# Instance normalization on one core: statistics halves summed on GpSimd, an early Sqrt table load, and g/b loads on ScalarE's queue

## The chip, the cores and the metric

The kernel runs on one core of one Trainium2 chip. The metric is the device time of one execution in microseconds. The profiler's span, from the first to the last instruction, is a little shorter than that time: 94.7 us for the kernel before, in a run of 96.55 us. All times below that belong to a point of the run count from the start of the span.

Names: VectorE is DVE, ScalarE is ACT, GpSimd is Pool, SyncE is SP. "Transfers" are the 16 DMA engines of the core.

## What is computed

Input x has shape (32, 576, 16, 32) in bf16: 32 x 576 = 18,432 images of 512 values. Each image is normalized by its own mean and variance and then scaled and shifted by its channel's g and b:

```python
mu = x.mean(axis=(-2, -1), keepdims=True)
var = ((x - mu) * (x - mu)).mean(axis=(-2, -1), keepdims=True)
xhat = (x - mu) / jnp.sqrt(var + 1e-5)
return xhat * g.reshape(1, -1, 1, 1) + b.reshape(1, -1, 1, 1)
```

x is 18.9 MB, and so is the output. Each value is read from HBM once and written once.

## The kernel before

**Tiling.** The 18,432 images are laid over 128 partitions, 144 images to a partition. A tile is one image on each partition: 128 x 512 bf16, 131 KB. All 144 tiles stay in SBUF, in the tensor `xs`, from the load to the store; nothing is evicted, and a tile is normalized in place.

**Loads.** SP issues 12 loads of 2, 2, 4, 8 and then 16 tiles each (table `ic`). Each has its own semaphore. Behind the first of them SP issues the loads of g and b, 36 KB each (L274, L275).

**Batches.** The tiles go in 13 batches of 3 to 18 tiles (table `bs`). The stages of one batch are:

1. Statistics, tile by tile. Most tiles go to DVE: `bn_stats` (L331) writes six numbers per image, a count, a mean and a sum of squared deviations for the even elements and again for the odd ones; `bn_aggr` (L333) turns the six into mean and variance in `mv`. The first `ka` tiles of a batch go to ACT instead: `p1` (L340) sums a tile with the accumulator, `p2` (L342) sums the squared deviations, and one small ACT operation per batch, `tiny` (L346), scales the means.
2. One Sqrt on ACT for the whole batch (L348), then one reciprocal on DVE (L335).
3. Three small operations on Pool, `tt1` to `tt3` (L353, L355, L357), which make `scale` = rstd x g and `bias` = b - mean x scale.
4. The normalization x scale + bias of each tile, on one of three engines: `na` tiles of a batch on ACT (L350), `nd` on DVE (L337), the rest on Pool (L359).
5. One store for the batch, which SP issues when all its tiles are normalized (L289).

**Order.** Each engine runs its instructions in the order in which they stand in its queue. The order isn't written out by hand. `build_ops` makes a list of operations with what each depends on; `simulate` is a small planner that runs through this list when the program is built, with a duration for each kind (`COST`), an arrival time for each load (`in_chunk_arrivals`) and a priority for each kind (`PRIO`), and puts each engine's operations in the order in which they would start. `emit_engine` then writes the instructions in that order. Where an operation depends on another, it waits for that engine's semaphore to reach the count of the operation that it needs. An instruction that waits holds up everything behind it on its engine.

The stores share SP's queue with the loads. All loads are issued by 9 us, before the first store at 12.48 us, and the transfers take them up in that order; so the first half of the run reads and the second half writes.

Of the kernel before, what the change touches and what calls it, by code (L numbers as in the profile page):

```python
# [9 lines left out]

COST = dict(
    bnstats=(594, 594), bnaggr=(68, 80), recip=(130, 252), normD=(323, 323),
    p1=(612, 612), p2=(705, 705), tiny=(190, 250), sqrt=(115, 216), normA=(702, 702),
    tt=(197, 222), normP=(742, 742),
)
NORM_CONTENDED = 785
HANDOFF = 90
HANDOFF_SAME = 100
DMA_TILE_NS = 306
DMA_FIRST = 1050  # L20
DMA_ISSUE = 380
DMA_SEM = 250
PRIO = dict(sqrt=0, tiny=1, recip=0, tt=0, bnaggr=2, normA=3, p2=4, p1=5, bnstats=5, normP=5, normD=6)


class Op:
    __slots__ = ("eng", "kind", "tile", "batch", "deps", "chunk", "busy", "lat", "start", "end", "done", "idx", "sub")

    def __init__(self, eng, kind, tile=None, batch=None, deps=(), chunk=None, sub=None):
        self.eng, self.kind, self.tile, self.batch = eng, kind, tile, batch  # L30
        self.deps = list(deps)
        self.chunk = chunk
        self.sub = sub
        key = "tt" if kind.startswith("tt") else kind
        self.busy, self.lat = COST[key]
        self.start = self.end = self.done = None
        self.idx = None

    def __repr__(self):
        return f"{self.eng}:{self.kind}(t={self.tile},b={self.batch})@{self.start}"  # L40


def in_chunk_arrivals(in_chunks, t0=0.0, n_pre_dmas=0):
    arr = []
    dma_free = 0.0
    issue_t = t0 + n_pre_dmas * DMA_ISSUE
    for (lo, hi) in in_chunks:
        issue_end = issue_t + DMA_ISSUE
        start = max(issue_t + DMA_FIRST, dma_free)
        end = start + (hi - lo) * DMA_TILE_NS  # L50
        dma_free = end
        arr.append(end + DMA_SEM)
        issue_t = issue_end
    return arr, dma_free, issue_t


def build_ops(n_tiles, batches, in_chunks):
# [5 lines left out]
    stat_done = {}  # L63
    for b, B in enumerate(batches):
        lo, hi, ka = B["lo"], B["hi"], B["ka"]
        p1s = []
        for i in range(lo, lo + ka):
            o1 = Op("A", "p1", tile=i, batch=b, chunk=chunk_of[i])
            o2 = Op("A", "p2", tile=i, batch=b, deps=[o1])
            ops += [o1, o2]  # L70
            p1s.append(o1)
            stat_done[i] = o2
        for i in range(lo + ka, hi):
            o1 = Op("D", "bnstats", tile=i, batch=b, chunk=chunk_of[i])
            o2 = Op("D", "bnaggr", tile=i, batch=b, deps=[o1])
            ops += [o1, o2]
            stat_done[i] = o2
        stats = [stat_done[i] for i in range(lo, hi)]
        tiny = None
        if ka > 0:  # L80
            tiny = Op("A", "tiny", batch=b, deps=p1s)
            ops.append(tiny)
        sq = Op("A", "sqrt", batch=b, deps=stats)
        rc = Op("D", "recip", batch=b, deps=[sq])
        t1 = Op("P", "tt1", batch=b, deps=[rc])
        t2 = Op("P", "tt2", batch=b, deps=[t1] + ([tiny] if tiny else []))
        t3 = Op("P", "tt3", batch=b, deps=[t2])
        ops += [sq, rc, t1, t2, t3]
        B["ops"] = dict(tiny=tiny, sqrt=sq, recip=rc, tt1=t1, tt2=t2, tt3=t3)
# [18 lines left out]
def simulate(ops, arrivals, t_start=0.0, verbose=False):  # L108
# [6 lines left out]

    def ready_time(o):
        r = t_start
        if o.chunk is not None:
            r = max(r, arrivals[o.chunk])
        for d in o.deps:  # L120
            if d.start is None:
                return None
            r = max(r, d.done + (HANDOFF_SAME if d.eng == o.eng else HANDOFF))
        return r

    n_left = len(ops)
    while n_left:
        best = None
        for e in "DAP":
            cands = []  # L130
            for o in pending[e]:
                r = ready_time(o)
                if r is not None:
                    cands.append((r, o))
            if not cands:
                continue
            tstar = max(free[e], min(r for r, o in cands))
            avail = [(PRIO["tt" if o.kind.startswith("tt") else o.kind], o.tile if o.tile is not None else -1, o.batch, r, o)
                     for r, o in cands if r <= tstar + 1e-9]
            avail.sort(key=lambda x: (x[0], x[2], x[1]))  # L140
            o = avail[0][4]
            if best is None or tstar < best[0]:
                best = (tstar, e, o)
        assert best is not None, "deadlock in schedule construction"
# [6 lines left out]
        o.start = tstar  # L151
        o.end = tstar + busy
        o.done = tstar + lat
# [12 lines left out]
def plan(n_tiles, batch_sizes, ka_list, na_list, nd_list, in_chunk_sizes, out_groups=None, verbose=False):  # L166
    batches = []
    lo = 0
    for G, ka, na, nd in zip(batch_sizes, ka_list, na_list, nd_list):
        batches.append(dict(lo=lo, hi=lo + G, ka=ka, na=na, nd=nd))  # L170
        lo += G
# [3 lines left out]
    for s in in_chunk_sizes:  # L175
        in_chunks.append((lo, lo + s))
        lo += s
    assert lo == n_tiles
    arrivals, dma_in_end, sp_free = in_chunk_arrivals(in_chunks, n_pre_dmas=0)
    ops = build_ops(n_tiles, batches, in_chunks)  # L180
    engs, free = simulate(ops, arrivals)
    if out_groups is None:
        out_groups = [(B["lo"], B["hi"]) for B in batches]
    norm_of = {}
# [5 lines left out]
    for (lo, hi) in out_groups:  # L190
# [9 lines left out]
    res = dict(batches=batches, in_chunks=in_chunks, arrivals=arrivals, engs=engs, free=free,  # L200
               out=out_info, total=total, dma_in_end=dma_in_end, out_groups=out_groups)
    return res


# [6 lines left out]
DEFAULT_TABLE = dict(  # L211
    bs=[3, 7, 10, 11, 15, 17, 18, 15, 15, 13, 12, 4, 4],
    ka=[2, 1, 2, 2, 4, 4, 4, 4, 4, 2, 2, 0, 0],
    na=[1, 2, 1, 1, 6, 4, 9, 5, 7, 7, 5, 1, 1],
    nd=[0, 0, 0, 0, 0, 0, 0, 0, 0, 0, 4, 3, 3],
    ic=[2, 2, 4, 8, 16, 16, 16, 16, 16, 16, 16, 16],
)


def bass_standalone__instancenorm__sampling_kernel(nc, x, g, b, out, table=None, NJUNK=4):  # L220
# [4 lines left out]
    assert NI % P == 0  # L225
# [5 lines left out]
    pl = plan(n, tb["bs"], tb["ka"], tb["na"], tb["nd"], tb["ic"], out_groups=tb.get("og"))  # L231
# [3 lines left out]
    out_groups = pl["out_groups"]  # L235

    c1 = -1.0 / (S * math.sqrt(S))
    c2 = 1.0 / math.sqrt(S)
    c3 = -math.sqrt(S)
# [4 lines left out]
    with ExitStack() as es:  # L244
# [8 lines left out]
        nms = sb("nms", [P, n], FP32)  # L253
# [4 lines left out]
        bias = sb("bias", [P, n], FP32)  # L258

# [4 lines left out]
        out_sem = sem("out_sem")  # L264
        block = es.enter_context(nc.Block())

        @block.sync
        def _(sp):
            gsrc = bass.AP(g.tensor, 0, [[0, P // q], [n, q], [1, n]])
            bsrc = bass.AP(b.tensor, 0, [[0, P // q], [n, q], [1, n]])  # L270
            for c, (lo, hi) in enumerate(in_chunks):
                sp.dma_start(xs[:, lo:hi, :], xv[:, lo:hi, :]).then_inc(in_sem[c], 16)  # L272
                if c == 0:
                    sp.dma_start(g_sb[:], gsrc).then_inc(g_sem, 16)  # L274
                    sp.dma_start(b_sb[:], bsrc).then_inc(b_sem, 16)  # L275
            norm_of = {}
            for Bt in batches:
                norm_of.update(Bt["norm"])
# [13 lines left out]
        def emit_engine(eng, E):  # L292
# [11 lines left out]
            for o in ops:  # L304
                assert o.idx == ops.index(o) if False else True
# [10 lines left out]
                lo, hi = Bt["lo"], Bt["hi"]  # L316
                i = o.tile
# [18 lines left out]
                elif k == "normD":  # L336
                    ins = eng.tensor_scalar(xs[:, i, :], xs[:, i, :], scale[:, i:i + 1], bias[:, i:i + 1],  # L337
                                            AluOpType.mult, AluOpType.add)
                elif k == "p1":
                    ins = eng.activation(jb, xs[:, i, :], ACTF.Identity, scale=c1, accum_out=nms[:, i:i + 1])  # L340
                elif k == "p2":
                    ins = eng.activation(jb, xs[:, i, :], ACTF.Square, bias=nms[:, i:i + 1], scale=c2,  # L342
                                         accum_out=mv[:, i, 1:2])
                elif k == "tiny":
                    ka = Bt["ka"]
                    ins = eng.activation(mv[:, lo:lo + ka, 0], nms[:, lo:lo + ka], ACTF.Identity, scale=c3)  # L346
                elif k == "sqrt":
                    ins = eng.activation(std[:, lo:hi], mv[:, lo:hi, 1], ACTF.Sqrt, bias=eps, scale=1.0)  # L348
                elif k == "normA":
                    ins = eng.activation(xs[:, i, :], xs[:, i, :], ACTF.Identity, bias=bias[:, i:i + 1],  # L350
                                         scale=scale[:, i:i + 1])
                elif k == "tt1":
# [5 lines left out]
                elif k == "normP":  # L358
                    ins = eng.tensor_scalar(xs[:, i, :], xs[:, i, :], scale[:, i:i + 1], bias[:, i:i + 1],  # L359
                                            AluOpType.mult, AluOpType.add)  # L360
                else:
                    raise AssertionError(k)
# [6 lines left out]
        @block.scalar  # L369
        def _(act):  # L370
            emit_engine(act, "A")

        @block.gpsimd
        def _(pool):
            emit_engine(pool, "P")
# [28 lines left out]
```

## Time and profile before

The median of three runs is 96.42 us (96.40 to 96.67).

| row | count | busy us | mean ns |
|---|---|---|---|
| DVE bn_stats (L331) | 113 | 73.9 | 666 |
| DVE bn_aggr (L333) | 113 | 17.5 | 162 |
| DVE normalization (L337) | 10 | 3.7 | 424 |
| ACT p1 (L340) | 31 | 19.0 | 615 |
| ACT p2 (L342) | 31 | 21.9 | 707 |
| ACT normalization (L350) | 50 | 36.8 | 800 |
| ACT table loads (L340, L348) | 2 | 2.6 | 1283 |
| Pool normalization (L359) | 84 | 63.8 | 780 |
| Pool tt1, tt2, tt3 (L353, L355, L357) | 39 | 8.9 | 225 to 234 |

The engines are busy for 79.9 us (DVE, 84% of the span), 82.3 (ACT, 87%) and 71.6 (Pool, 76%). The queue that SP feeds takes 95.9% of the time of the 16 DMA engines.

How to read it: the mean of a row is the time of one instruction from its start to its end, and on DVE and ACT an instruction begins before the end of the one ahead of it. The distance from start to start, called the pitch below, is what an instruction costs in a queue. The timeline gives it: bn_stats 0.58 us and bn_aggr 0.08 on DVE, p1 0.61 and p2 0.70 on ACT, a normalization 0.70 on ACT and 0.75 on Pool.

### The profile page before, as it was taken

Reading aid. Unit: us, or ns where it says so; the run is one execution under the profiler, and the core shown is the slowest. Engines: PE = TensorE matmul, PEld = TensorE weight load, DVE = VectorE, ACT = ScalarE, POOL = GpSimd, SP = SyncE. Lnnn points to the kernel's source line nnn. Section 1 sums busy time; section 2 is a strip of 40 time slices with the busy share of each in tenths; the row PEclk is TensorE's granted clock in tenths of the full one; section 3 lists DMA queues with packets and bytes.
Section 4 is the critical chain, followed back from the end, with each engine's and each line's share of the span. In section 5 each row is a group of like instructions: output and inputs, shape, how many; then the busy total and the mean of one; then the engine's idle time right before and its main releaser. Section 6 shows DMA issues by size and latency. Waiting matters only on the chain.

```text
span 94.7 us, 659 instructions
## 1 busy us (share of the span) xinstructions
DVE 79.9 (84%) x249; ACT 82.3 (87%) x200; POOL 71.6 (76%) x127
## 2 busy tenths in 40 slices
DVE  0039597999999999999999999999999999999100
ACT  5598397989999999999999999999999999899000
POOL 0000807959999999999999999999999999895000
DMA  1799999999999999999999999999999999899995
GB/s 29 208 348 394 436 415 443 429 415 436 436 429 429 436 422 422 439 422 422 436 381 439 429 428 438 441 442 419 433 436 420 432 393 422 344 413 399 420 403 211
DMA packets 3894, 37.87 MB, mean 400 GB/s; under 512 B 689, under 2 KB 689, under 8 KB 1585
## 3 DMA queue, kind: packets, MB, share of 16 engines
q1 hardware_dynamic: 3888, 37.82, 95.9%
q14 instruction: 6, 0.04, 0.1%
HBM read 18.95 MB, written 18.87 MB: 399 GB/s over the span
## 4 chain that ended last, share of the span: by engine, by line
DVE 76%; DMA 12%; SPq 3%; issue 0%; DVEq 0%; ACT 0%
DVE bnst L331 62%; DMA xs<-in_x_dram 12%; DVE mv L333 8%; DVE xs L337 3%; SPq L272 2%; DVE rstd L335 2%; SPq L274 1%; SPq L275 1%; DVEq L244 0%; ACT std L348 0%
## 5 line engine op out<-in xcount | busy, mean ns | idle before, releaser
L331 DVE BATCH_NORM_STATS2 bnst<-xs 128x6 f32<-128x512 bf16 x113 | 73.9, 666 | 7.9 <-DMA xs<-in_x_dram 7.9
L359 POOL TENSOR_SCALAR xs<-xs,scale,bias 128x512 bf16<-128x512 bf16 x84 | 63.8, 780 | 1.1
L350 ACT ACTIVATE xs<-xs,bias,scale 128x512 bf16<-128x512 bf16 x50 | 36.8, 800 | 1.0 <-POOL bias L357 0.9
L342 ACT ACTIVATE junk<-xs,nms 128x512 bf16<-128x512 bf16 x31 | 21.9, 707 | 0.0
L340 ACT ACTIVATE junk<-xs 128x512 bf16<-128x512 bf16 x31 | 19.0, 615 | 3.2 <-DMA xs<-in_x_dram 3.2
L333 DVE BATCH_NORM_AGGREGATE mv<-bnst 128x2 f32<-128x6 f32 x113 | 17.5, 162 | 0.1
L353 POOL TENSOR_TENSOR scale<-rstd,g_sb 128x15 f32<-128x15 f32 (+9 forms) x13 | 3.0, 230 | 12.7 <-DVE mv L333 12.5
L340 ACT ACTIVATION_READ_ACCUMULATOR junk<-xs 128x1 f32 x31 | 5.8, 187 | 0.0
L342 ACT ACTIVATION_READ_ACCUMULATOR junk<-xs,nms 128x1 f32 x31 | 5.8, 187 | 0.0
L337 DVE TENSOR_SCALAR xs<-xs,scale,bias 128x512 bf16<-128x512 bf16 x10 | 3.7, 424 | 0.0
L357 POOL TENSOR_TENSOR bias<-b_sb,tmp 128x15 f32<-128x15 bf16 (+9 forms) x13 | 2.9, 225 | 0.7
L355 POOL TENSOR_TENSOR tmp<-mv,scale 128x15 f32<-128x15 f32 (+9 forms) x13 | 3.0, 234 | 0.5
L348 ACT ACTIVATE std<-mv 128x15 f32<-128x15 f32 (+9 forms) x13 | 2.6, 200 | 0.4 <-DVE mv L333 0.4
L335 DVE RECIPROCAL rstd<-std 128x15 f32<-128x15 f32 (+9 forms) x13 | 2.8, 213 | 0.2 <-ACT std L348 0.2
L346 ACT ACTIVATE mv<-nms 128x2 f32<-128x2 f32 (+2 forms) x11 | 2.1, 195 | 0.0
L340 ACT ACT_TABLE_LOAD x1 | 1.3, 1283 | 0.7 <-PEq L389 0.7
L348 ACT ACT_TABLE_LOAD x1 | 1.3, 1283 | 0.0
L389 POOL MEMSET const-float32-0.0<- 128x1 f32 x1 | 0.1, 99 | 0.2 <-issue 0.2
L389 POOL MEMSET const-bfloat16-1.0<- 128x1 bf16 x1 | 0.1, 102 | 0.0
L389 POOL MEMSET const-uint8-127<- 128x1 uint8 x1 | 0.1, 102 | 0.0
L389 POOL MEMSET const-float32-1.0<- 128x1 f32 x1 | 0.1, 99 | 0.0
## 6 DMA issues: line engine op xcount, KB each, us to landing
xs<-in_x_dram SPq DMA_DIRECT2D x8, 2048.0 KB, 26.7
out_dram<-xs SPq DMA_DIRECT2D x3, 1920.0 KB, 9.8
out_dram<-xs SPq DMA_DIRECT2D x1, 2304.0 KB, 13.1
out_dram<-xs SPq DMA_DIRECT2D x1, 2176.0 KB, 15.5
out_dram<-xs SPq DMA_DIRECT2D x1, 1664.0 KB, 5.9
out_dram<-xs SPq DMA_DIRECT2D x1, 1536.0 KB, 5.5
out_dram<-xs SPq DMA_DIRECT2D x1, 1408.0 KB, 23.4
out_dram<-xs SPq DMA_DIRECT2D x1, 1280.0 KB, 28.2
```

The costliest lines, as they stand in the source:

```text
L331: ins = eng.bn_stats(bnst[:, i, :], xs[:, i, :])
L333: ins = eng.bn_aggr(mv[:, i, :], bnst[:, i, :])
L335: ins = eng.reciprocal(rstd[:, lo:hi], std[:, lo:hi])
L337: ins = eng.tensor_scalar(xs[:, i, :], xs[:, i, :], scale[:, i:i + 1], bias[:, i:i + 1], AluOpType.mult, AluOpType.add)
L340: ins = eng.activation(jb, xs[:, i, :], ACTF.Identity, scale=c1, accum_out=nms[:, i:i + 1])
L342: ins = eng.activation(jb, xs[:, i, :], ACTF.Square, bias=nms[:, i:i + 1], scale=c2, accum_out=mv[:, i, 1:2])
L348: ins = eng.activation(std[:, lo:hi], mv[:, lo:hi, 1], ACTF.Sqrt, bias=eps, scale=1.0)
L350: ins = eng.activation(xs[:, i, :], xs[:, i, :], ACTF.Identity, bias=bias[:, i:i + 1], scale=scale[:, i:i + 1])
L353: ins = eng.tensor_tensor(scale[:, lo:hi], rstd[:, lo:hi], g_sb[:, lo:hi], AluOpType.mult)
L355: ins = eng.tensor_tensor(tmp[:, lo:hi], mv[:, lo:hi, 0], scale[:, lo:hi], AluOpType.mult)
L357: ins = eng.tensor_tensor(bias[:, lo:hi], b_sb[:, lo:hi], tmp[:, lo:hi], AluOpType.subtract)
L359: ins = eng.tensor_scalar(xs[:, i, :], xs[:, i, :], scale[:, i:i + 1], bias[:, i:i + 1], AluOpType.mult, AluOpType.add)
```

## The change

It has four parts.

1. **bn_aggr is replaced for most batches.** For a batch marked "p" in a new table `agg`, the two halves that `bn_stats` wrote are put together for the whole batch at once, in six small operations. Pool adds the halves (`P1`: the sum of the means and of the squared deviations, in `pa`) and subtracts the means (`P2`: `dd`). ACT squares the difference with the right factor (`sq`: `qq`) and halves the sum of the means (`mh`). Pool adds `qq` and the summed squared deviations (`P4`). Sqrt then divides by the count through its scale. Batches marked "d" keep bn_aggr. ACT's own statistics tiles now write mean and summed squares in the form that this Sqrt takes, and `tiny` goes.
2. **The Sqrt table is loaded first.** Pool sets one value, and ACT takes its square root ahead of all else, so that the table set with Sqrt is loaded at the start and not at the first batch's Sqrt.
3. **g and b are loaded from ACT's queue**, behind that warm-up, and not from SP's between the first x loads.
4. **New tables and planner figures.** There are ten batches of 3 to 25 tiles in place of 13, other shares for the engines, loads of 1, 2, 4, 8, 17 and then 16 tiles, and a store for each batch as before. The planner's costs change a little, and it takes a load's semaphore as 1000 ns late in place of 250.

It is meant to relieve DVE of the aggregation, and to bring the first x loads and the first Sqrt forward.

```diff
 def build_ops(batches, in_chunks):
...
         for i in range(dlo, hi):
             o1 = Op("D", "bnstats", tile=i, batch=b, chunk=chunk_of[i])
...
+            if agg == "d":
+                o2 = Op("D", "bnaggr", tile=i, batch=b, deps=[o1])
...
+        if agg == "p":
+            if bns:
+                P1 = Op("P", "P1", batch=b, deps=bns)
+                P2 = Op("P", "P2", batch=b, deps=bns)
+                sq = Op("A", "sq", batch=b, deps=[P2])
+                mh = Op("A", "mh", batch=b, deps=[P1])
+                P4 = Op("P", "P4", batch=b, deps=[sq, P1])
...
+            sqr = Op("A", "sqrt", batch=b, deps=[P4] + p2s)
...
-DEFAULT_TABLE = dict(
-    bs=[3, 7, 10, 11, 15, 17, 18, 15, 15, 13, 12, 4, 4],
-    ka=[2, 1, 2, 2, 4, 4, 4, 4, 4, 2, 2, 0, 0],
-    na=[1, 2, 1, 1, 6, 4, 9, 5, 7, 7, 5, 1, 1],
-    nd=[0, 0, 0, 0, 0, 0, 0, 0, 0, 0, 4, 3, 3],
-    ic=[2, 2, 4, 8, 16, 16, 16, 16, 16, 16, 16, 16],
-)
+DEFAULT_TABLE = {"bs": [3, 11, 20, 25, 21, 17, 16, 16, 9, 6], "ka": [0, 0, 9, 4, 3, 3, 1, 1, 1, 0],
+                 "na": [1, 0, 5, 10, 8, 12, 10, 7, 3, 2], "nd": [0, 0, 0, 0, 0, 0, 0, 3, 6, 4],
+                 "agg": ["p", "d", "p", "p", "p", "p", "p", "p", "p", "d"],
+                 "ic": [1, 2, 4, 8, 17, 16, 16, 16, 16, 16, 16, 16]}
...
             for c, (lo, hi) in enumerate(in_chunks):
                 sp.dma_start(xs[:, lo:hi, :], xv[:, lo:hi, :]).then_inc(in_sem[c], 16)
-                if c == 0:
-                    sp.dma_start(g_sb[:], gsrc).then_inc(g_sem, 16)
-                    sp.dma_start(b_sb[:], bsrc).then_inc(b_sem, 16)
...
                 elif k == "p1":
-                    ins = eng.activation(jb, xs[:, i, :], ACTF.Identity, scale=c1, accum_out=nms[:, i:i + 1])
+                    ins = eng.activation(jb, xs[:, i, :], ACTF.Identity, scale=inv_s, accum_out=mv[:, i, 0:1])
...
+                elif k == "sq":
+                    ins = eng.activation(qq[:, dlo:hi], dd[:, dlo:hi], ACTF.Square, scale=sq_scale)
+                elif k == "mh":
+                    ins = eng.activation(mv[:, dlo:hi, 0], pa[:, dlo:hi, 0], ACTF.Identity, scale=0.5)
...
+                elif k == "P1":
+                    ins = eng.tensor_tensor(pa[:, dlo:hi, :], bnst[:, dlo:hi, 1:3], bnst[:, dlo:hi, 4:6], AluOpType.add)
+                elif k == "P2":
+                    ins = eng.tensor_tensor(dd[:, dlo:hi], bnst[:, dlo:hi, 1], bnst[:, dlo:hi, 4], AluOpType.subtract)
+                elif k == "P4":
+                    ins = eng.tensor_tensor(mv[:, dlo:hi, 1], qq[:, dlo:hi], pa[:, dlo:hi, 1], AluOpType.add)
...
         def _(act):
+            act.wait_ge(warm_sem, 1)
+            act.activation(warm[:, 1:2], warm[:, 0:1], ACTF.Sqrt)
+            if gb_q == "scalar":
+                gb_loads(act)
             emit_engine(act, "A")
...
         def _(pool):
+            pool.memset(warm[:, 0:1], 1.0).then_inc(warm_sem, 1)
...
             emit_engine(pool, "P")
```

## The prediction

> **What bounds the kernel now.** I read the busy slices first, because they show all engines and the transfers against one clock.
>
> ```profile
> DVE  0039597999999999999999999999999999999100
> ACT  5598397989999999999999999999999999899000
> POOL 0000807959999999999999999999999999895000
> DMA  1799999999999999999999999999999999899995
> ...
> HBM read 18.95 MB, written 18.87 MB: 399 GB/s over the span
> ```
>
> Each digit is 2.4 us. The chain of waits names VectorE for 76% of the span, but the transfers are busy earlier than VectorE and five slices longer. So I asked for the transfers by stretch:
>
> ```profile
> 2.00:5.00 3.00, 0.00 (x0) 1.58 (x6) 0.00 (x0) 1.00 0.76 201
> ...
> 20.00:48.00 28.00, 28.00 (x88) 28.00 (x77) 27.35 (x46) 1.00 1.01 429
> 48.00:52.00 4.00, 4.00 (x15) 4.00 (x15) 4.00 (x6) 1.00 0.98 408
> 52.00:77.00 25.00, 24.82 (x78) 24.84 (x56) 24.53 (x42) 1.00 1.01 433
> 77.00:83.00 6.00, 6.00 (x20) 5.75 (x11) 5.63 (x11) 1.00 0.87 370
> ```
>
> The columns are the stretch, its length, busy DVE, ACT and POOL, clock, transfer share and GB/s. The transfers run full (share 1.01) from 20 to 77 us: this is a DMA-bound kernel with two leaks. All loads stand in the queue by 9 us, so the reads run first. Summing the GB/s column by microsecond, 18.41 MB have moved at 47 us and the last read at about 48.25 us; then the writes run, at 131 KB / 433 GB/s = 0.303 us a tile. Ideally 144 tiles take 43.6 us, 91.9 us as the end. Data in fact ends at 93.6 us, and the leak is in 77 to 83 us: (433-370) x 6 / 433 = 0.9 us. The timeline shows why:
>
> ```profile
> 80.04 2.21 ACT L350 ACTIVATE xs<-xs,bias,scale 128x512 bf16<-128x512 bf16 x3
> ...
> 82.32 6.47 SPq L289 DMA_DIRECT2D out_dram<-xs  x4
> ```
>
> A 13-tile store was issued at 82.32, when ACT's last normalization of that batch ended at 82.25; its first bytes moved at 83.0. So **a batch that is ready later than 0.75 us before the previous store drains costs idle transfer time.** The engines matter through that alone. The other leak is the start:
>
> ```profile
> 1.18 0.61 SPq L274 DMA_DIRECT2D g_sb<-in_g_dram  x1
> 1.84 0.59 SPq L275 DMA_DIRECT2D b_sb<-in_b_dram  x1
> 2.47 6.75 SPq L272 DMA_DIRECT2D xs<-in_x_dram  x11
> ```
>
> The loads of g and b sit between the first and second x loads. From 3.00 to 4.25 us only 96 GB/s move, at a share of 0.60.
>
> **What the Trainium skill says.** "DMA: Bandwidth & Descriptors", section "Queues, rings and completion order": SP and ACT each have their own ring on the same 16 DMA engines, served in turn. So g and b on ACT's queue leave SP's issue order but not the DMA engines; the trace of before has no ACT queue to compare. "ScalarE: Activation LUTs", section "What ACT_TABLE_LOAD costs": 1283 ns; both loads here took 1283. "SBUF — State Buffer", section "Who interferes with whom": a DVE operation with at most one SBUF input outside the two-port modes does not contend with GpSimd. The trace agrees: bn_stats keeps 0.58 us a tile beside a busy Pool.
>
> **The change part by part.** *g/b off SP's queue, first chunk one tile.* The second x load issues at about 0.73+0.45 = 1.18 instead of 2.47, 1.29 us earlier. That is the most the stream can gain. Against it, the g/b packets now run inside the stream; 1.25 us x 0.60 = 0.75 us bounds their engine time, so the least is 0.54. I take 0.8. The g wait before Pool's first scale is about 8 us into the run; g landed 2.4 us after issue before, so even issued at 2.2 us (after the warm table load) it is there.
>
> *Table.* Sqrt's set is loaded first and serves Identity and Square: before, the second load ran at 6.9 us; after has one. Saves 1.28 us of ACT, worth nothing: ACT then waits for the fifth chunk, below.
>
> *Work moved.* The tables give 122 bn_stats (113), 17 bn_aggr (113), 13 DVE normalizations (10); 22 ACT statistics tiles (31), 58 ACT normalizations (50); 73 Pool normalizations (84), and 54 small Pool operations (39). By the pitches in the timeline (bn_stats 0.583, aggr 0.08, DVE norm 0.32; ACT 0.61+0.705 and 0.704; Pool 0.752): DVE +5.2-7.7+1.0 = -1.5, and about -2 with three fewer reciprocals; ACT -11.8+5.6, and 16 small operations more, 14 fewer at 0.11 (+0.2) = -6.0, -1.3 table; Pool -8.3 + 15 x 0.25 = -4.5. The changed scales of the ACT statistics and the write of the mean straight into its place cost nothing: same shapes. Three stores fewer (10 against 13) save SP's issues of 0.33 us, which lie beside running transfers. All three engines lose work. But the profile says busy time is not the measure; readiness against the stores is.
>
> *Where the engines start.* The order of the changed kernel has ka=0 in the first two batches: ACT gets one tile, then waits for the fifth chunk, ending at tile 32 in both kernels. DVE started on that chunk at 15.87 before; so 15.07 after. ACT then has 21 x 1.315 + 57 x 0.704 + 23 x 0.11 = 70.3 us, so it can't end before 85.4 (87.7 before). Pool: batch 1's reciprocal stands behind the first bn_stats of that chunk on DVE, so its scale starts at 15.8 and its normalizations at 16.7.
>
> *What is queued behind the new waits.* The new path per batch is Pool's two sums, ACT's Square, Pool's sum, Sqrt: four crossings. Each Pool sum stands behind up to six normalizations, and ACT's Square behind it holds ACT's normalizations. Walking the order with the pitches above (Pool sums 0.25, the pair 0.5; the nearest row is tmp at 230 ns; 128x42 might be 0.35) gives few stops: ACT about 1 us in all, Pool 1.3 at 26 us (scale behind a Sqrt that follows eight ACT tiles). Ready times, and stores from 47.45 (48.25-0.8), plus 0.2 for the dip at 48 to 52:
>
> | store (tiles) | last producer | ready | previous drained | lost | drained |
> |---|---|---|---|---|---|
> | 3 (25), tile 59 | Pool | 53.5 | 57.95 | 0 | 65.55 |
> | 4 (21) | Pool | 65.35 | 65.55 | 0.55 | 72.45 |
> | 5 (17) | Pool | 69.75 | 72.45 | 0 | 77.6 |
> | 6 (16) | ACT | 77.55 | 77.6 | 0.7 | 83.15 |
> | 7 (16) | ACT, DVE | 82.75 | 83.15 | 0.35 | 88.35 |
> | 8 (9) | DVE, ACT | 85.0 | 88.35 | 0 | 91.1 |
> | 9 (6) | ACT | 86.4 | 91.1 | 0 | 92.9 |
>
> "Lost" is ready + 0.75 - drained. Store 4's Pool line: 16.7 + 1.3 idle + 54 x 0.752 + 26 x 0.25 = 65.1, and 0.2 for the hand-offs. Store 6's ACT line: 15.07 + 21 x 1.315 + 45 x 0.704 + 18 x 0.11 = 76.35, and about 1 of stops, which the walk puts at 77.55. With 0.3 us of tail, as before (83.0 + 33 x 0.303 + 0.3 for the gap at 87 gives 93.3 against 93.6), data ends at 93.2. Sum: start -0.8; leaks of 1.6 instead of 0.9 and 0.3, +0.4. So 96.42 - 0.4 = **96.0 us**. The removed bn_aggr is thus worth almost nothing on the path: DVE gets nine more tiles, and ACT's normalizations end the stores.
>
> **The rivals.** *No wait at all*: the ready times are pessimistic by over 0.7 us, and the stream runs through: 47.45 + 0.2 + 43.6 + 0.3 = 91.55, 2.0 less: 94.4. For it: margins at all other stores and less work everywhere. Against: ACT's plain sum of work already gives store 6. *New hand-offs cost more*: an extra 0.1 us at each of 12 ACT crossings up to store 7 gives 1.2 more: 97.2, **slower**. For it: ACT now waits on Pool twice a batch, and Pool's spans in a profile are rough; against: the waits table of before puts ACT's wait on Pool at 0.9 us in all. *No gain at the start*: g/b on the second ring take as much from the small chunks as they took before, gain 0.1: 96.7.
>
> **How the numbers follow.** Main case 0.48 (95.4 to 96.5, by the start's 0.54 to 1.29 and pitches), no wait 0.19, hand-offs 0.23, no start gain 0.10. Faster: 0.36 + 0.19 + 0.01 = 0.56. Same (96.13 to 96.71): 0.12 + 0.01 + 0.06 = 0.19. Slower: 0.22 + 0.03 = 0.25. The range 94.5 to 97.2 leaves out about half of the no-wait case and the worse half of the hand-offs.
>
> **What would show it.** Right: transfers at full share from about 2 us; DVE's wait for the fifth chunk ends near 15.1; transfer share under 1 near 66, 78 and 83 us, each before a store whose issue follows Pool or ACT; last normalization near 86.4. Wrong: a full share to the end (then 94.4), or ACT idle over 2 us on Pool's sums (then slower), or the fifth chunk at 15.8.

## The result and the profile after

The changed kernel takes 95.26 us (median of 12 runs, 94.99 to 95.93). In the same comparison the kernel before takes 96.89 us at the median; the ratio is 0.9845, with a 95% interval of 0.9812 to 0.9878. That is about 1.5 us less. The forecast was 0.4 us less (96.0, range 94.5 to 97.2). The comparisons leave disturbed runs out; the profiles of experiments 4 and 13 are of such runs (97.76 and 97.54 us) and serve only to show when loads land and stores are issued.

The busy slices of the kernel after, 2.33 us to a digit in a span of 93.3 us:

```profile
DVE  0388898999999999999999999999999999994000
ACT  6020807999999999999999999999999999996000
POOL 1022602999929999999999999999999999630000
DMA  1999999999999999999999999999999999989996
```

The second digit of the transfers was 7 and is 9: they are full sooner. At the other end DVE shows no work in the last three slices, against the last two before: the engines are done a little further ahead of the last transfers.

The same stretches as in the prediction (stretch, length, busy DVE, ACT, POOL, clock, transfer share, GB/s):

```profile
2.00:5.00 3.00, 1.14 (x2) 0.22 (x2) 0.00 (x0) 1.00 0.92 266
...
20.00:48.00 28.00, 28.00 (x51) 28.00 (x76) 26.01 (x46) 1.00 1.00 427
48.00:52.00 4.00, 4.00 (x8) 4.00 (x11) 4.00 (x9) 1.00 1.05 443
52.00:77.00 25.00, 24.89 (x46) 24.97 (x49) 24.64 (x48) 1.00 1.00 430
77.00:83.00 6.00, 5.80 (x21) 6.00 (x13) 4.48 (x12) 1.00 0.97 414
```

The middle has not changed (429 to 427 and 433 to 430 GB/s). Both leaks are smaller: the start moves 266 GB/s for 201, and 77 to 83 us moves 414 for 370.

The issues at the start, and the two instructions that began on the fifth load (timeline):

```profile
0.73 6.97 SPq L307 DMA_DIRECT2D xs<-in_x_dram  x12
0.74 1.28 ACT L412 ACT_TABLE_LOAD   x1 [0.74 <-PEq L436]
0.87 0.62 ACTq L301 DMA_DIRECT2D g_sb<-in_g_dram  x1
1.52 0.62 ACTq L302 DMA_DIRECT2D b_sb<-in_b_dram  x1
...
14.77 0.63 ACT L371 ACTIVATE junk<-xs 128x512 bf16<-128x512 bf16 x1
```

```profile
14.77 0.69 DVE L362 BATCH_NORM_STATS2 bnst<-xs 128x6 f32<-128x512 bf16 x1 [0.34 <-DMA xs<-in_x_dram]
```

The fifth load is used at 14.77 us, against 15.87 in the kernel before:

```profile
15.87 1.29 DVE L331 BATCH_NORM_STATS2 bnst<-xs 128x6 f32<-128x512 bf16 x2 [0.57 <-DMA xs<-in_x_dram]
```

In the changed kernel DVE waited only 0.34 us for it. One profile does not fix this point: with the same start it is used at 15.45, 15.21 and 14.73 us in the profiles of experiments 3, 7 and 8.

And the end, where the prediction expected ACT to hold the stores:

```profile
73.72 4.32 ACT L387 ACTIVATE xs<-xs,bias,scale 128x512 bf16<-128x512 bf16 x6
76.70 0.33 SPq L320 DMA_DIRECT2D out_dram<-xs  x1
```

ACT's last normalizations of batch 6 are the first four of these six; they start 0.70 us apart and take 0.80, so the fourth ends at 76.63, just before the store's issue at 76.70. So ACT is the last producer, as forecast, but 0.85 us sooner.

The table sets each store's forecast against the trace. "Drained" is the point at which the store ahead has moved its bytes, found by adding the GB/s column in steps of 0.25 us, backwards from the last byte; it is good to 0.25 us. "In hand" is the time from a store's issue to that point. Where the transfers pause, the count from behind finds the first bytes of the next store instead, so a late store too shows about 0.75 here. "Lost" is therefore read from the packets of the trace, each of which has a start and a duration: it is the time in which some of the 16 DMA engines had no packet, counted as a share of all 16.

| store | ready, forecast | issued | previous drained, forecast | measured | in hand | lost, forecast | measured |
|---|---|---|---|---|---|---|---|
| 4 | 65.35 | 64.59 | 65.55 | 65.6 | 1.0 | 0.55 | 0 |
| 5 | 69.75 | 68.93 | 72.45 | 72.0 | 3.0 | 0 | 0 |
| 6 | 77.55 | 76.70 | 77.6 | 77.5 | 0.8 | 0.7 | 0.18 |
| 7 | 82.75 | 81.92 | 83.15 | 82.75 | 0.8 | 0.35 | 0.16 |
| 8 | 85.0 | 84.10 | 88.35 | 87.5 | 3.4 | 0 | 0 |
| 9 | 86.4 | 85.51 | 91.1 | 90.4 | 4.9 | 0 | 0 |

Two of the three forecast waits came, and both were shorter. From 77.1 to 77.7 us the number of engines with a packet falls to 9, from 82.5 to 82.9 us to 4. Together that is 0.34 us of the transfers' time and not 1.6. The same count gives 0.65 us for the kernel before: 0.14 near 77.6 us and 0.51 from 82.4 to 83.3 us. The stretch from 82 to 84 us, before and then after, shows the longer pause and the shorter one in the transfers' share:

```profile
82.00:84.00 2.00, 2.00 (x9) 1.75 (x4) 1.82 (x4) 1.00 0.66 278
```

```profile
82.00:84.00 2.00, 2.00 (x8) 2.00 (x4) 0.76 (x3) 1.00 0.85 360
```

### The profile page after: what moved, and what is told of

It is laid out like the page before. It is cut to its first block, busy times and chain, and to the rows that moved or that the text cites. A ratio compares the mean times of both kernels' runs of the same rounds, so it can differ in the third digit from the quotient of the medians.

```text
span 93.3 us, 548 instructions
## 1 busy us (share of the span) xinstructions
DVE 79.6 (85%) x162; ACT 75.1 (81%) x174; POOL 66.3 (71%) x132
## 4 chain that ended last, share of the span: by engine, by line
DVE 36%; POOL 22%; ACT 17%; DMA 13%; SPq 2%; ACTq 1%; issue 1%
DVE bnst L362 35%; POOL xs L368 19%; ACT xs L387 16%; DMA xs<-in_x_dram 13%; SPq L307 2%; ACTq L271 1%; DVE rstd L366 1%; POOL scale L396 1%; POOL tmp L398 1%; POOL bias L400 1%; POOL pa L390 0%; POOL mv L394 0%; ACT mv L378 0%; ACT std L381 0%; POOL dd L392 0%
## 5 line engine op out<-in xcount | busy, mean ns | idle before, releaser
L368 POOL TENSOR_SCALAR xs<-xs,scale,bias 128x512 bf16<-128x512 bf16 x73 | 56.3, 794 | 0.6
L387 ACT ACTIVATE xs<-xs,bias,scale 128x512 bf16<-128x512 bf16 x58 | 42.5, 798 | 0.0
L371 ACT ACTIVATE junk<-xs 128x512 bf16<-128x512 bf16 x22 | 13.5, 614 | 2.6 <-DMA xs<-in_x_dram 2.5
L373 ACT ACTIVATE junk<-xs,mv 128x512 bf16<-128x512 bf16 x22 | 15.5, 706 | 0.0
L396 POOL TENSOR_TENSOR scale<-rstd,g_sb 128x16 f32<-128x16 f32 (+8 forms) x10 | 2.4, 243 | 9.3 <-DVE rstd L366 6.1
L373 ACT ACTIVATION_READ_ACCUMULATOR junk<-xs,mv 128x1 f32 x22 | 4.1, 186 | 0.0
L400 POOL TENSOR_TENSOR bias<-b_sb,tmp 128x16 f32<-128x16 bf16 (+8 forms) x10 | 2.5, 245 | 0.5
L398 POOL TENSOR_TENSOR tmp<-mv,scale 128x16 f32<-128x16 f32 (+8 forms) x10 | 2.4, 242 | 0.5
L366 DVE RECIPROCAL rstd<-std 128x16 f32<-128x16 f32 (+8 forms) x10 | 2.3, 234 | 0.3 <-ACT std L381 0.2
L364 DVE BATCH_NORM_AGGREGATE mv<-bnst 128x2 f32<-128x6 f32 x17 | 2.5, 161 | 0.0
```

The costliest lines, as they stand in the source:

```text
L364: ins = eng.bn_aggr(mv[:, i, :], bnst[:, i, :])
L366: ins = eng.reciprocal(rstd[:, lo:hi], std[:, lo:hi])
L371: ins = eng.activation(jb, xs[:, i, :], ACTF.Identity, scale=inv_s, accum_out=mv[:, i, 0:1])
L373: ins = eng.activation(jb, xs[:, i, :], ACTF.Square, bias=mv[:, i, 0:1], scale=-1.0, accum_out=mv[:, i, 1:2])
L396: ins = eng.tensor_tensor(scale[:, lo:hi], rstd[:, lo:hi], g_sb[:, lo:hi], AluOpType.mult)
L398: ins = eng.tensor_tensor(tmp[:, lo:hi], mv[:, lo:hi, 0], scale[:, lo:hi], AluOpType.mult)
```

## The experiments

Three readings were set against each other. **R**: two gains, one from the earlier x stream and one from batches that are ready in time. **S**: the start is the whole gain. **N**: the batches are the whole gain. Ratios below are to the kernel before, in the same comparison; for the changed kernel it is 0.9845, and 0.001 is about 0.1 us.

### 1. The new batches with the old place of g and b

```diff
-                if c == 2 and gb_q == "sync":
+                if c == 0 and gb_q == "sync":
...
-... NJUNK=4, gb_q="scalar"):
+... NJUNK=4, gb_q="sync"):
```

> The changed kernel with the loads of g and b back on SP's queue between the first and the second x load; all else as changed. Theory R (two gains: the x stream starts about 0.6 us earlier, and the new batches are ready before the transfers run dry, worth about 0.9): 0.5 to 0.8 us slower than the changed kernel, near 95.9. Rival S (the early start is the whole gain, since every engine starts earlier with it): back to the time before, 1.4 us slower. Rival N (the batches are the whole gain): no change.

Measured: 96.79 us, ratio 1.0018 (0.9996 to 1.004), 1.7 us above the changed kernel. Reading S holds here, and R and N fall: **without the early start, the new batches and the sums on Pool bring nothing.** The trace agrees with S's mechanism in part. Start of the fifth load's use:

```profile
2.44 6.25 SPq L307 DMA_DIRECT2D xs<-in_x_dram  x11
...
15.83 0.69 DVE L362 BATCH_NORM_STATS2 bnst<-xs 128x6 f32<-128x512 bf16 x1 [0.42 <-DMA xs<-in_x_dram]
```

That is 1.06 us later than 14.77, and every later store follows: store 6 is issued at 77.76 (76.70), store 7 at 82.98 (81.92). The stream is as late: by 20 us it has moved 6,632 KB against 7,072 in the changed kernel, 440 KB or 1.03 us. Stream and engines move together, so the stores are no later against the transfers: their pauses cost 0.40 us here and 0.34 in the changed kernel. The other 0.7 us of this profile's longer span lies at the very end:

```profile
93.50:94.00 0.50, 0.00 (x0) 0.00 (x0) 0.00 (x0) 1.00 0.07 25
```

A share of 0.07 is about one of the 16 engines (1/16 is 0.0625). One engine still moves data from 93.6 to 94.3 us when the others have none left; in the changed kernel all 16 end within 0.15 us. Why one ends late is not shown.

### 2. No early table load

```diff
-            act.wait_ge(warm_sem, 1)
-            act.activation(warm[:, 1:2], warm[:, 0:1], ACTF.Sqrt)
...
-            pool.memset(warm[:, 0:1], 1.0).then_inc(warm_sem, 1)
```

> The changed kernel without the early Sqrt, so that there are two table loads again. Theories R and S: no change within 0.2 us, as ACT stands idle until the fifth load lands at 14.8 us and the first store has no use before 48 us. Rival T (the first batch's delay of 1.3 us carries on along Pool and ACT): 0.5 to 1.3 us slower.

Measured: 95.44 us, ratio 0.9881 (0.984 to 0.9923). The middle is 0.35 us above the changed kernel, but 0.9845 lies within the interval: not told from no change, though the lower end of T's 0.5 us is not excluded either. The trace speaks for none: ACT starts on the fifth load at 14.75 us, as with the early load, and the last store is issued at 85.25 us (85.51).

### 3. The aggregation back on DVE

```diff
-                 "agg": ["p", "d", "p", "p", "p", "p", "p", "p", "p", "d"],
+                 "agg": ["d"] * 10,
```

> The changed kernel with its new tables, but bn_aggr on DVE for every batch. DVE gets 105 aggregations at 0.082 us, 8.6 us; Pool loses 24 small operations. Theory R: DVE had about 1.7 us to spare ahead of Pool's first sum in batches 6 and 7, so stores 6 and 7 come about 5 us later: 99 to 101 us, slower than before the change. Rival (the place of the aggregation does not matter, Pool and ACT set the stores): within 1 us of the changed kernel.

Measured: 101.58 us, ratio 1.0528 (1.0484 to 1.0573): 6.6 us above the changed kernel, a little more than expected. The stretches at the end:

```profile
75.00:80.00 5.00, 5.00 (x19) 3.84 (x7) 1.11 (x3) 1.00 0.70 300
80.00:85.00 5.00, 5.00 (x16) 4.28 (x7) 4.74 (x9) 1.00 0.87 367
85.00:90.00 5.00, 5.00 (x20) 3.36 (x8) 1.68 (x7) 1.00 0.12 52
```

DVE is full, ACT and Pool wait, and the transfers stand at a share of 0.12: store 7 is issued at 88.89 us instead of 81.92. So with the new tables, which give DVE nine more tiles, the sums on Pool are needed to keep the stores in time. They are a condition of the gain, not its source.

### 4. The kernel before with g and b on ACT's queue and the early table load

```diff
-                if c == 0:
-                    sp.dma_start(g_sb[:], gsrc).then_inc(g_sem, 16)
-                    sp.dma_start(b_sb[:], bsrc).then_inc(b_sem, 16)
...
         def _(act):
+            act.wait_ge(warm_sem, 1)
+            act.activation(warm[:, 1:2], warm[:, 0:1], ACTF.Sqrt)
+            act.dma_start(g_sb[:], gsrc).then_inc(g_sem, 16)
+            act.dma_start(b_sb[:], bsrc).then_inc(b_sem, 16)
```

> The kernel before with only the new start: g and b on ACT's queue behind an early Sqrt; tables and bn_aggr as before. Theory R: the x stream gains about 0.6 us and the engines start with it, so 0.5 to 0.8 us faster than before. Rival S: the full 1.4 us. Rival N: no change, as the batch of 13 tiles at 82 us comes when DVE and Pool have it ready, whatever the start.

Measured: 96.87 us, ratio 1.0024 (0.999 to 1.0058): no gain, as N had it; R and S both expected one. In its profile the fifth load is used at 16.45 us, which is no earlier than before (15.87), though g and b no longer stand between the loads. Both the sizes of the first loads and the batches are still the old ones here, so this run doesn't say which of the two keeps the gain away. Experiment 11 takes up the sizes.

### 5 and 6. The transfers alone

Both kernels are reduced to their loads and stores, the changed one in experiment 5 and the one before in experiment 6; the edit is the same, shown for the changed kernel.

```diff
-                for e, v in need.items():
-                    if v > waited[e]:
-                        sp.wait_ge(sem_e[e], v)
+                for c, (clo, chi) in enumerate(in_chunks):
+                    if clo < hi and chi > lo and c not in wc:
+                        sp.wait_ge(in_sem[c], 16)
...
-            emit_engine(act, "A")
```

> The transfers of the changed kernel alone: same loads, g and b on ACT's queue, same ten stores, each waiting only for its loads; no statistics and no normalization, so the output is x itself. This is the floor that the transfers set. Theory R: the changed kernel loses little to late stores, so 0.3 to 0.9 us under it, 94.4 to 95.0. Rival (the engines still hold the stores up by several us): 93.5 or less.

> The transfers of the kernel before alone: its loads with g and b between the first two, its thirteen stores, each waiting only for its loads; no statistics and no normalization. Theory R: the late start stays and the late stores go, so about 0.6 us above the transfers of the changed kernel alone and 1.2 to 1.5 us under the kernel before. Rival (the new, larger stores move faster by themselves): 1 us or more above the other transfers.

Measured: 95.15 us, ratio 0.9851 (0.9801 to 0.99), for the changed kernel's transfers; 96.29, ratio 0.997 (0.9943 to 0.9998), for those of before. **The changed kernel stands on its floor** (95.26 against 95.15), as far as intervals of about 0.5 us to each side can tell. The kernel before stood 0.3 us above its own. R had expected 0.3 to 0.9 us for the first distance and 1.2 to 1.5 for the second; both came out smaller. The rival's 93.5 us or less for experiment 5 is ruled out. So of the gain of 1.5 us about 1.2 is the floor itself, and only about 0.3 is late stores that are gone. Stretches of the first, for comparison with the table above (its columns are ACT, POOL, clock, share, GB/s):

```profile
20.00:48.00 28.00, 0.00 (x0) 0.00 (x0) 1.00 1.00 427
...
52.00:77.00 25.00, 0.00 (x0) 0.00 (x0) 1.00 1.01 436
```

With no engine at work, loads run at the same 427 GB/s and stores at 436 for 430. By 20 us the new transfers have moved 6,967 KB and the old 6,805, which is 0.4 us. When 37.0 of the 37.8 MB have moved, the old ones are 0.6 us behind. The other 0.5 us lies in the last 0.8 MB, where the 16 engines don't end together: idle engines cost 1.02 us of the transfers' time at the end of experiment 6 and 0.52 at the end of experiment 5.

The same count explains how a kernel with 0.34 us of pauses can stand on its floor: with no engine at work no store waits, but the end is uneven (0.52 us); in the changed kernel the end costs only 0.08. These counts are of one profile each.

### 7 and 8. Two more operations on ACT, two more on DVE

```diff
+                if E == "A" and k == "normA" and o.batch == 4 and not dummy_done:
+                    dummy_done.append(1)
+                    for t in range(2):
+                        eng.activation(d_out[:, t, :], d_in[:], ACTF.Identity)
```

```diff
+                if E == "D" and k == "bnstats" and o.batch == 5 and not dummy_done:
+                    dummy_done.append(1)
+                    for t in range(2):
+                        eng.bn_stats(d_st[:, t, :], d_in[:])
```

> The changed kernel with two more ACT operations of a tile's size (0.61 us each without a bias operand, 1.2 us together) ahead of batch 4's first normalization, on a tile of zeros. Theory R (Pool and then ACT are the last to make stores 6 and 7 ready, with almost no slack): 0.6 to 1.2 us slower. Rival (the transfers alone set the time): no change.

> The changed kernel with two more bn_stats on DVE (0.583 us each, 1.2 us) ahead of batch 5's first, on a tile of zeros. Theory R: DVE is about 1.7 us ahead of Pool's first sum from batch 5 on, so nothing up to 0.3 us. Rival D (the DVE chain still sets the end): 1.2 us slower.

Measured: 96.35 us, ratio 0.9952 (0.9931 to 0.9972), for ACT, 1.0 us more than the changed kernel; 95.68, ratio 0.99 (0.9863 to 0.9938), for DVE, 0.5 us more. ACT went as R expected. Three stretches of that trace:

```profile
65.00:66.00 1.00, 1.00 (x3) 1.00 (x5) 1.00 (x3) 1.00 0.60 256
...
78.00:79.00 1.00, 1.00 (x4) 1.00 (x2) 1.00 (x3) 1.00 0.66 280
...
84.00:85.00 1.00, 1.00 (x4) 1.00 (x2) 0.24 (x1) 1.00 0.61 262
```

The transfers starve near 66, 78 and 84 us, the three places where the prediction had put its waits (66, 78, 83). These rows book a packet wholly where it starts, which blurs the edges; counted by packets the pauses are 0.30, 0.57 and 0.27 us, 1.14 in all against 0.34. Stores 6 and 7 are issued at 77.77 and 82.99, 1.07 us later, of which 0.44 comes from a fifth load that is used at 15.21 in this profile. (The edit also has Pool write the tile of zeros first, so that g is issued at 1.33 us and not at 0.87.) A shift of 1.07 us costs 1.0 us: these two stores have next to nothing to spare.

For DVE the expectation was too low. The two operations were put ahead of a reciprocal on DVE, and this row of the trace shows what waited for it:

```profile
48.69 0.23 POOL L405 TENSOR_TENSOR scale<-rstd,g_sb 128x21 f32<-128x21 f32 x1 [0.73 <-DVE rstd L375]
```

DVE has time to spare in its statistics, but not in the small operations of the chain that stand in its queue. Stores 3 to 7 all come about 0.55 us later, and the pauses are 0.59 us against 0.34.

### 10 and 11. Which part of the transfers

Both are the transfers of experiment 5 with one part put back: the thirteen stores, or the old first loads.

```diff
+            out_groups = [(0,3),(3,10),(10,20),(20,31),(31,46),(46,63),(63,81),(81,96),(96,111),(111,124),(124,136),(136,140),(140,144)]
```

```diff
-                 "ic": [1, 2, 4, 8, 17, 16, 16, 16, 16, 16, 16, 16]}
+                 "ic": [2, 2, 4, 8, 16, 16, 16, 16, 16, 16, 16, 16]}
```

> The transfers of the changed kernel alone, but in the thirteen stores of the kernel before (two last stores of four tiles); no statistics and no normalization. Theory F (the change lowered the floor of the transfers by 1.1 us, half by the start and half by ten stores in place of thirteen): 0.4 to 0.7 us slower than the transfers with ten stores, near 95.7. Rival G (the start alone lowered the floor): no change, near 95.15.

> The transfers of the changed kernel alone, but with loads of 2, 2, 4, 8, 16 tiles as before; g and b stay on ACT's queue, ten stores; no statistics and no normalization. Theory F: the place of g and b makes the start, the sizes of the first loads little: within 0.2 us of 95.15. Rival H (the sizes of the first loads make the start, as the kernel before with g and b on ACT's queue had gained nothing): 0.3 to 0.6 us slower.

Measured: 95.04 us, ratio 0.983 (0.9793 to 0.9867), with thirteen stores: no change, so theory F falls and the number of stores is no part of the lower floor. With the old loads 96.13 us, ratio 0.9926 (0.99 to 0.9952): 0.7 us above experiment 5, where F had expected no more than 0.2 and H 0.3 to 0.6. **In the transfers alone the sizes of the first loads are the larger part of the lower floor.** The rest, 0.997 - 0.9926 or 0.4 us, falls to the place of g and b, with intervals that overlap. The two parts do not simply add: experiment 1 kept the new sizes and lost 1.7 us with the place alone.

Experiment 11's profile is one of its fastest runs (95.55), and there the stream is no later than in experiment 5 (7,033 KB at 20 us). What it loses, it loses at the end: the uneven end costs 1.08 us of the transfers' time, much as in experiment 6 (1.02), against 0.52 and 0.42 in experiments 5 and 10, which have the new loads. Why the old loads should leave the engines less even is open. Its times are spread over 1.8 us (95.20 to 96.97), those of experiment 5 over 0.9.

### 12 and 13. Two other starts

```diff
+                if c == 1:
+                    continue
...
+            lo1, hi1 = in_chunks[1]
+            act.dma_start(xs[:, lo1:hi1, :], xv[:, lo1:hi1, :]).then_inc(in_sem[1], 16)
             act.wait_ge(warm_sem, 1)
```

```diff
-... NJUNK=4, gb_q="scalar"):
+... NJUNK=4, gb_q="sync"):
```

> The changed kernel with its second x load issued first on ACT's queue, ahead of g and b, so that two x loads are issued at once and the later ones 0.45 us earlier. Theory F (the transfers are the floor and the start counts one for one): 0.2 to 0.5 us faster than the changed kernel. Rival: the small packets of g and b now fall among larger loads and take it back, no change.

> The changed kernel with g and b on SP's queue behind the third x load, where seven tiles (2.1 us of transfers) are queued ahead of them. Theory F: the x stream never starves at the start, and g and b cost their 0.56 us of packets either way: within 0.3 us of the changed kernel. Rival S (any place on SP's queue costs what the old place costs): 1.5 us slower, as with g and b between the first two loads.

Measured: 95.42 us, ratio 0.9857 (0.9829 to 0.9886), for the second load on ACT's queue: no change, the rival held. By 5 us this start has moved 975 KB against 837, by 20 us 7,020 against 7,072. g landed 5.1 us and b 10.9 us after issue, and the first store came at 14.73 us (11.09 in the changed kernel). With g and b behind the third load: 96.70 us, ratio 0.9974 (0.9947 to 1.0001), 1.25 us above the changed kernel. F falls; SP's queue costs nearly the whole gain at this place too, though seven tiles are queued ahead.

The profile of this run shows where. By 20 us 7,020 KB have moved, hardly less than in the changed kernel, and yet the fifth load is used late:

```profile
16.11 0.69 DVE L362 BATCH_NORM_STATS2 bnst<-xs 128x6 f32<-128x512 bf16 x1 [0.32 <-DMA xs<-in_x_dram]
```

That is 1.34 us after 14.77, and stores 6 and 7 are issued 1.34 us later too. Most packets of this load are in time: half of its 128 have ended by 11.65 us (11.61 in the changed kernel) and nine tenths by 13.67 (13.56). The last ends at 15.74, against 14.40. **A load can be used when its last packet has landed, and the bytes moved don't show that.**

## Why the prediction was right, and where it was not

**What bounds it: right.** Experiment 5 shows it: the kernel after is at the floor of its transfers. The 0.75 us rule held in the main: in the changed kernel the stores with 1.0 us or more in hand lost nothing, stores 6 and 7 with 0.8 lost a little, and experiment 7 made the transfers starve where it took that away. But the rule treats the transfers as one. The packets show 16 engines that run dry one after another, over 0.9 us in the kernel before. The slices were misread at one point: the transfers outlast DVE by two to three slices, not by five.

**The start: the term was 0.8 us, the stream shows 0.57.** 7,072 KB against 6,830 by 20 us are 242 KB, at 428 GB/s 0.57 us, just above the lower bound of 0.54. It is one pair of profiles; five others with the same start (experiments 3, 5, 7, 8 and 10) moved 6,891 to 7,037 KB, a gain of 0.1 to 0.5 us. Measured as time the start counts for more: the floor fell by 1.2 us, and experiment 1 put only the place of g and b back and lost 1.7. Its first load is one tile and not two, so less moves ahead of the gap; its stream is 1.03 us late and not 0.57. I had also taken "first chunk one tile" and "g/b off the queue" as one edit of one size, and looked at bytes alone. Experiments 4 and 11 show that the second without the first brings nothing measurable in the full kernel with the old batches, and that the first is the larger of the two in the transfers alone. Experiment 13 shows that a stream with nearly the same bytes can deliver a load 1.34 us later.

**The term that failed: "leaks of 1.6 instead of 0.9 and 0.3".** The leaks measured 0.34 after and 0.65 before, so a term of +0.4 us was really -0.3. The 1.6 was too much because the ready times were 0.75 to 0.9 us too late, against drained times that were right to 0.4 us for the three stores in question. Two terms make that up. The smaller is the fifth load, used at 14.77 and not 15.07; this lies within the scatter of the profiles (14.73 to 15.45), so the forecast of 15.07 was not wrong in itself. The larger is the stops in ACT's walk, "about 1 us in all", which were 0.4: from 14.77 to ACT's end at 85.49 are 70.7 us, against 70.3 of plain work. Pool's stop came where it was forecast (1.62 us at 27 us, for 1.3). The leak of before was over-read too: by packets the 0.9 from the GB/s column is 0.51, the gap at 87 us isn't there, and a pause of 0.14 us near 77.6 was missed. Experiment 6 without any engine is only 0.3 us faster.

**The number.** Both terms were off in the same direction, the start by about 0.4 us against the floor and the leaks by 0.7. That 95.26 lies within the range is owed to the range, which was drawn wide for the rival without waits, and not to the sum of 96.0.

**The rivals.** "No wait at all" comes nearest to the trace; its 94.4 was too low, since 0.34 us of waits stayed and the stream gained less than 0.8 us at the start; the rest is not accounted for. "Hand-offs cost more" failed: the table of waits names none of ACT for Pool after the first batch. "No gain at the start" is what happened to g and b on ACT's queue alone (experiment 4). The table load at no cost stands within experiment 2's error. "The removed bn_aggr is worth almost nothing on the path" was half of it: with these tables it is worth 6.6 us, since without it DVE sets the stores.

**Open:** how the sizes of the first loads act, and why the 16 engines end unevenly; and the old batches with the whole new start, which was not run, so that it is not shown how much of the gain the old batches would have kept.

## What to carry to other kernels

Where the transfers are full from end to end, run them alone before re-balancing the engines: here that floor held 1.2 us of a gain of 1.5, and the kernel before had only 0.3 us above its own. Judge a new division of the engines by what each store has in hand when the store ahead drains, since the sums on Pool were needed (6.6 us without them) and still not the source of the gain. The first few loads of a stream, their sizes and what stands between them, deserve the same care as the last store. Judge them by when a load's last packet lands, not by the bytes moved.

## What the runs showed of the hardware

A load issued from ACT's queue did not wait for ACT's table load: g went out at 0.87 us while the table load ran from 0.74 to 2.02. Small loads beside a full stream land at very different times: g and b, 36 KB each, took 2.4 and 2.6 us on SP's queue before, 3.3 and 3.2 us on ACT's queue after, and 5.1 and 10.9 us in experiment 12. A change of ACT's table set took 1.28 us in all: in experiment 2 the operation before it ends at 6.62 us, the load runs from 6.64 to 7.92, and Sqrt starts at 7.94. The 16 DMA engines of a core do not finish a queue together: in the transfers alone all 16 are busy until 91.7 us and the last ends at 92.5 (experiment 5), and in experiment 1 one engine runs 0.7 us longer than the other fifteen. Statistics and normalization on three engines took little from the transfers: 427 GB/s of loads and 430 of stores with them, 427 and 436 without.
